# Real 2-D FFT into a squared-ReLU FFN on one Trainium2 core: folds split over two blocks, Nyquist matmuls at the block's end, a row spread by way of DRAM, changed steps by load

## The chip, the cores and the metric

One core of a Trainium2 chip runs the whole kernel. The metric is the device time of one execution in microseconds. Five engines work from queues of their own: TensorE (PE in the profile, its weight loads PEld), VectorE (DVE), ScalarE (ACT), GpSimd (POOL) and SyncE (SP), which issues the stores and the transfer changed here.

## The reference

`x` is 8 x 3008 x 256. The tokens are the real part of its 2-D FFT over sequence and width, and each goes through a feed-forward network with a squared ReLU:

```
X = np.fft.fft(np.fft.fft(x, axis=1), axis=2).real      # 8 x 3008 x 256
t = X.reshape(24064, 256)
h = np.maximum(t @ w_in, 0.0)                           # w_in  256 x 2048
out = (h * h) @ w_out                                   # w_out 2048 x 256
```

## The kernel before

Cosine and sine symmetries shrink the transform. The sequence is folded by VectorE (sums and differences of mirrored rows and columns), and the width transform is multiplied into `w_in` once (`gh`). What is left per batch are the cosine part `zc` and the sine part `zs`, 128 rows each, one column for a pair of mirrored frequencies k and S-k. Of a pair, one token's hidden value is P + Q and the other's P - Q, with P = `gh[:,0]` times `zc` and Q = `gh[:,1]` times `zs`. Row 0 of `zs` is an exception: it carries the component d=128, which enters both tokens with the same sign.

The 12,040 columns are cut into 25 **blocks** (`wins`; counted from 0; 240, 512, 376, 376, 512 and 448 columns, then 512 each, the last 360). A block has eight **steps** of 2 x 128 hidden units. The order of the work is written out by hand, one program order for each engine:

- A **plain step** (`pq`, `square`, `turn`): four matmuls give P + Q in a bank `ph`, ScalarE takes the ReLU, VectorE or (steps in `by_act`) ScalarE squares it into `h2`; two more matmuls with `gh[:,2]` turn the bank into P - Q, and the same follows for the mirrored token.
- A **changed step** (`half_q`, `half_p`, listed by `halved`): two matmuls give Q, ScalarE copies -2Q to `sn`, two matmuls add P, ScalarE copies the sum to `hd`, and VectorE makes P - Q from the two. Row 0's part must not change sign, so VectorE adds back `wv` times `eb`: `eb` is row 0 of `zs` on all 128 partitions, brought by `row_spread` (line 580), which SyncE issues at the head of step 7 of the block before.
- Between the two halves of each step, `others(s)` runs a share of the block before's second matmul (`ffn2_steps`, line 617, sums in `po`, evicted to `osb` at line 632 and stored by SyncE at line 597), of the transform whose columns begin in the next block (`z_steps`, line 481, with the difference `minus` on VectorE, line 497), and the jobs of `at[s]` and `post[s]`.
- The **fold** of batch i >= 2 stands in a **fold block** (`fold_at`: 5, 8, 10, 13, 16, 19): `d_even`, `n_cos`, `d_odd`, `n_sin`, `odds` in steps 0 to 4, then `nyq` (two small matmuls `py`, lines 376 and 377, that read `od` from `odds`) at step 5, `even` (which writes the scratch `scr`) at 6 and `back` (which reads it into `rb`) at 7. `d_odd` also issues the loads of the next batch's `x` on GpSimd. The fold of the odd-even part, `late`, stands in steps 2 to 5 of another block (`late_at`: 6, 9, 12, 15, 18, 21).
- `halved` gives blocks of 512 columns from block 6 on the changed steps 1, 2, 4 and 5, fold blocks 1 and 3; all others none.

Of the kernel before, what the change touches and what calls it, by code (L numbers as in the profile page):

```python
# [9 lines left out]
F16 = mybir.dt.float16  # L10
I32 = mybir.dt.int32
AF = mybir.ActivationFunctionType
ALU = mybir.AluOpType

HS = 32.0
P = 128
# [3 lines left out]
def rev_dim(ap, i):  # L20

    dims = [list(d) for d in ap.ap]
    step, cnt = dims[i]
    dims[i] = [-step, cnt]
    return bass.AP(tensor=ap.tensor, offset=ap.offset + step * (cnt - 1), ap=dims)
# [3 lines left out]
def kernel(  # L29
# [14 lines left out]
    nc = tc.nc  # L44
# [10 lines left out]
    WN = 512  # L55
# [1 line left out]
    FIRST = [240, 512, 376, 376, 512, 448]  # L57
    R23 = float(2.0 ** 23)

    MANY, FEW = (1, 2, 4, 5), (1, 3)  # L60
    SQ_MANY, SQ_FEW = (0, 3, 6), (0, 4, 6)

    RQ = (1, 3, 5, 0, 2, 4)

# [11 lines left out]
    wins = []  # L76
# [5 lines left out]
    NW = len(wins)  # L82
# [29 lines left out]
    drp = ctx.enter_context(tc.tile_pool(name="drp", bufs=2, space=bass.MemoryType.DRAM))  # L112
# [172 lines left out]
    at = const.tile([P, 2, P + 1], F32, name="at")  # L285
# [169 lines left out]
    def zwin(w):  # L455
        if w not in zc:
            zc[w] = zp.tile([P, WN], F16, name="zc", tag="zc")
            zs[w] = zp.tile([P, WN], F16, name="zs", tag="zs")
        return zc[w], zs[w]
# [104 lines left out]
    wv = small([P, NFC], "wv")  # L564
# [8 lines left out]
    eb = {}  # L573

    def row_spread(w):

        wn = wins[w][1]
        t = eb[w] = tmp.tile([P, WN], F16, name="eb", tag="kf")
        src = zwin(w)[1][0:1, 0:wn]
        nc.sync.dma_start(out=t[:, 0:wn], in_=bass.AP(tensor=src.tensor, offset=src.offset, ap=[list(src.ap[0]), [0, P], [1, wn]]))  # L580

    def store(osb, p0, g0, m, minus, eng=nc.sync):

# [65 lines left out]
    folds = {0: f0s}  # L649

    def fold_jobs(i):
        f = folds[i] = fold_steps(i)
        return [f["d_even"], f["n_cos"], f["d_odd"], f["n_sin"], f["odds"], f["nyq"], f["even"], f["back"]]

    fold_at, late_at = {}, {}
# [2 lines left out]
        late_at[win_of(col_of[i, 1]) - 2] = i  # L658
    NST = NFC // 2

    def halved(w):

        if wins[w][1] < WN or w < 6:
            return ()
        return FEW if w in fold_at else MANY

    ROT = [0]
    old = None
    for w in range(NW):
        g0, wn = wins[w]  # L670
        h2 = h2p.tile([P, NFC, 2 * WN], F16, name="h2", tag="h2")
        zcw, zsw = zwin(w)

        lo, hi = 0, NST - 1
        at = [[] for _ in range(NST)]
        post = [[] for _ in range(NST)]
        if w == 0:
            at[2] = [f0s["even"], f0s["back"]]
        elif w == 1:
            fj = fold_jobs(1)  # L680
            at = [[f] for f in fj[0:5]] + [[], [], []]
            post[5] = fj[5:6]
            lo, hi = 6, 7
        elif w == 2:
            te = table_steps(1)
            at = [[folds[1]["even"], lambda: te["freq"](), lambda: te["args"](0)], [lambda: te["turns"](0)], [lambda: te["mods"](0)],
                  [lambda: te["absm"](0)], [lambda: te["sins"](0)], [lambda: te["coss"](0)], [], [lambda: te["weigh"]()]]
            for st in range(4):
                at[st + 3] = at[st + 3] + f0s["late"][st : st + 1]
            at[7].append(folds[1]["back"])  # L690
        elif w in fold_at:
            fj = fold_jobs(fold_at[w])
            at = [[f] for f in fj[0:5]] + [[], fj[6:7], fj[7:8]]
            post[5] = fj[5:6]
        elif w == win_of(col_of[1, 1]) - 1:
            for st in range(4):
                at[st] = folds[1]["late"][st : st + 1]
            lo = 4
        if w in late_at:
            for st in range(4):  # L700
                at[st + 2] = at[st + 2] + folds[late_at[w]]["late"][st : st + 1]
        if w == 3:
            at[0].append(row_weights)
        zj, zl = [], []
        for u in need[w + 1]:
            zu = z_steps(u)
            zj += [(zu, 0, 0), (zu, 1, 0), (zu, 0, 1), (zu, 1, 1)]
        f2 = ffn2_steps(*old) if old else []
        phs = {}

        def pq(s):
            ph = phs[s] = ps_h.tile([P, 2, 512], F32, name="ph", tag="psh")
            for a in range(2):
                f0 = (2 * s + a) * P
                nc.tensor.matmul(ph[:, a, 0:wn], gh[:, 0, f0 : f0 + P], zcw[:, 0:wn], start=True, stop=False)  # L715
                nc.tensor.matmul(ph[:, a, 0:wn], gh[:, 1, f0 : f0 + P], zsw[:, 0:wn], start=False, stop=True)  # L716

        def turn(s):
            for a in range(2):
                f0 = (2 * s + a) * P  # L720
                nc.tensor.matmul(phs[s][:, a, 0:wn], gh[:, 2, f0 : f0 + P], zsw[:, 0:wn], start=False, stop=True, skip_group_check=True)  # L721

        def square(s, sg):
            h1 = h1p.tile([P, 2, 512], F16, name="h1", tag="h1")
            nc.scalar.activation(h1[:, :, 0:wn], phs[s][:, :, 0:wn], AF.Relu)  # L725
            hv = rev_dim(h1[:, :, 0:wn], 2) if sg else h1[:, :, 0:wn]
            if sg == 0 and s in by_act:
                nc.scalar.activation(h2[:, 2 * s : 2 * s + 2, 0:wn], hv, AF.Square)  # L728
            else:
                nc.vector.tensor_tensor(h2[:, 2 * s : 2 * s + 2, sg * wn : (sg + 1) * wn], hv, hv, op=ALU.mult)  # L730

        two = halved(w)
        by_act = () if not two else SQ_FEW if w in fold_at else SQ_MANY
        sns, hds = {}, {}

        def half_q(s):
            ph = phs[s] = ps_h.tile([P, 2, 512], F32, name="ph", tag="psh")
            for a in range(2):
                f0 = (2 * s + a) * P
                nc.tensor.matmul(ph[:, a, 0:wn], gh[:, 1, f0 : f0 + P], zsw[:, 0:wn], start=True, stop=True)  # L740
            i = ROT[0] % 2
            sn = sns[s] = const.tile([P, 2, 2, WN], F16, name=f"sn{i}", tag=f"w16_{i}")
            nc.scalar.activation(sn[:, 0, :, 0:wn], ph[:, :, 0:wn], AF.Copy, bias=0.0, scale=-2.0)  # L743
            for a in range(2):
                nc.vector.tensor_scalar(out=sn[:, 1, a, 0:wn], in0=eb[w][:, 0:wn], scalar1=wv[:, 2 * s + a : 2 * s + a + 1], scalar2=None, op0=ALU.mult)  # L745
            nc.vector.tensor_tensor(sn[:, 0, :, 0:wn], sn[:, 0, :, 0:wn], sn[:, 1, :, 0:wn], op=ALU.add)  # L746

        def half_p(s):
            ph, sn = phs[s], sns[s]
            for a in range(2):  # L750
                f0 = (2 * s + a) * P
                nc.tensor.matmul(ph[:, a, 0:wn], gh[:, 0, f0 : f0 + P], zcw[:, 0:wn], start=False, stop=True, skip_group_check=True)  # L752
            hd = tmp.tile([P, 2, 2 * WN], F16, name="hd", tag=("tt", "tm")[ROT[0] % 2])
            ROT[0] += 1
            nc.scalar.activation(hd[:, :, 0:wn], ph[:, :, 0:wn], AF.Copy, bias=0.0, scale=1.0)  # L755
            nc.vector.tensor_tensor(rev_dim(hd[:, :, wn : 2 * wn], 2), hd[:, :, 0:wn], sn[:, 0, :, 0:wn], op=ALU.add)  # L756
            nc.vector.tensor_scalar(out=hd, in0=hd, scalar1=0.0, scalar2=None, op0=ALU.max)  # L757
            nc.vector.tensor_tensor(h2[:, 2 * s : 2 * s + 2, :], hd, hd, op=ALU.mult)  # L758

        def others(s):  # L760
            for j in at[s]:
                j()
            for j in spread(f2, s, NST):
                j()
            for j in post[s]:
                j()
            if s == lo:
                zl[:] = [j for zu, part, h in zj for j in zu(part, h)]
            if s >= lo:
                for j in spread(zl, s - lo, hi - lo) if s < hi else []:  # L770
                    j()


        ng = 2 if w == 0 or wins[w - 1][1] < 384 < wn else 1
        for s0 in range(0, NST, ng):
            ss = range(s0, s0 + ng)
            if s0 == hi and w + 1 < NW and halved(w + 1):
                row_spread(w + 1)
            if s0 in two:
                half_q(s0)  # L780
                others(s0)
                half_p(s0)
                continue
            for s in ss:
                pq(s)
            for s in ss:
                square(s, 0)
            others(s0)
            for s in ss:
                turn(s)  # L790
            for s in ss:
                square(s, 1)
            for s in ss[1:]:
                others(s)
        old = (w, h2)
    for j in ffn2_steps(*old, tail=True):
        j()
# [30 lines left out]
```

## Time and profile before

| | |
|---|---|
| median of 3 runs | 635.52 us (635.35 to 637.25) |
| profiled execution | 632.15 us, span 630.0 us, mean granted TensorE clock 0.992 |
| busy: PE, ACT, DVE, POOL | 596.5, 511.2, 475.5, 80.8 us |
| matmuls `po` (L617) | 3024 |
| plain steps, changed steps | 138, 62 |
| transfers | 49.89 MB, mean 79 GB/s |

Matmuls overlap in the profile, so their busy time and their mean duration are longer than the distance from one start to the next. A bracket at the end of a timeline row gives the engine's idle time before it and what ended it. "A <- B" in the table of waits says that A stood idle until B was done. In the windows view each row is a stretch of the span: its length, the busy time of each engine with the number of instructions, the granted clock, the share of the DMA engines and their rate.

### The profile page before, as it was taken

The page shows a single profiled execution, that of the slowest core. Times are in us where ns is not written, and L with a number is a line of the kernel's source. Part 1 is how long each engine was busy: PE and PEld are TensorE (multiplying, and loading weights), DVE is VectorE, ACT ScalarE, POOL GpSimd, SP SyncE. Part 2 cuts the span into 40 slices and gives each one's busy share as a digit, 9 for nine tenths or more (in the row PEclk, how much of TensorE's full clock was granted, in tenths as well). Part 3 has the DMA queues.
Part 4 walks back from the last instruction along what each step waited for, and adds up shares of the span by engine and source line. Part 5 has one row for each costly group of instructions (what it writes and reads, how often), then busy time and mean ns, then how long its engine had stood idle before and what let it go on. Part 6 is the DMA issues. An engine that isn't in the chain of part 4 may idle for free.

```text
span 630.0 us, 11638 instructions
## 1 busy us (share of the span) xinstructions
PE 596.5 (95%) x4440; PEld 428.5 (68%) x4440; DVE 475.5 (75%) x799; ACT 511.2 (81%) x664; POOL 80.8 (13%) x125
## 2 busy tenths in 40 slices
PE   5899999999899999899999999999996999999997
PEld 2457786776577677577776777766774677777786
DVE  7887655766799688867997779959787587886830
ACT  7787778779798888789888898888896689899762
POOL 5352200022000210210003200022000200000000
PEclk9999999999999999899999999999999899999999
DMA  8936211174313823743137533264322313413112
GB/s 148 211 80 129 85 34 34 50 142 110 31 54 57 169 80 52 144 92 57 52 45 116 136 59 42 61 119 122 49 39 68 72 65 43 55 49 39 58 53 66
DMA packets 39118, 49.89 MB, mean 79 GB/s; under 512 B 4503, under 2 KB 32919, under 8 KB 39063
## 3 DMA queue, kind: packets, MB, share of 16 engines
q1 hardware_dynamic: 29491, 26.80, 22.2%
q0 software_dynamic: 9344, 22.14, 17.4%
q8 instruction: 34, 0.56, 0.4%
q10 hardware_dynamic: 228, 0.21, 0.1%
q14 instruction: 21, 0.17, 0.1%
HBM read 33.63 MB, written 27.84 MB: 98 GB/s over the span
## 4 chain that ended last, share of the span: by engine, by line
PE 51%; DVE 19%; ACT 11%; issue 8%; DMA 8%; POOL 2%; ACTq 0%; DVEq 0%; POOLq 0%
PE po L617 29%; ACT h L725 5%; PE ph L721 5%; PE ph L715 5%; PE ph L716 5%; DVE h L730 3%; PE ph L752 3%; DVE h L758 3%; DMA out_dram<-osb 3%; DMA eb<-zs 2%; PE ph L740 2%; DVE hd L757 2%; DVE hd L756 2%; PE pz L481 2%; DVE fo L356 2%
## 5 line engine op out<-in xcount | busy, mean ns | idle before, releaser
L617 PE MATMUL po<-wout,h 128*128 128x256 f16 (+1 forms) x3024 | 363.2, 273 | 0.0
L617 PEld LDWEIGHTS <-h 128*128 128x128 f16 (+1 forms) x3024 | 297.6, 99 | 72.6 <-issue 1.1
L725 ACT ACTIVATE h<-ph 128x1024 f16<-128x1024 f32 (+4 forms) x276 | 253.2, 951 | 46.6 <-PE ph L721 31.5
L730 DVE TENSOR_TENSOR h<-h 128x1024 f16<-128x1024 f16 (+4 forms) x222 | 137.1, 632 | 93.0 <-ACT h L725 89.6
L716 PE MATMUL ph<-zs,gh 128*128 128x512 f16 (+4 forms) x276 | 99.9, 364 | 3.1 <-DVE zs L497 2.7
L715 PE MATMUL ph<-zc,gh 128*128 128x512 f16 (+4 forms) x276 | 99.9, 364 | 1.1 <-ACT h L725 0.8
L721 PE MATMUL ph<-zs,gh 128*128 128x512 f16 (+4 forms) x276 | 76.7, 363 | 1.9 <-ACT h L725 1.5
L632 ACT ACTIVATE osb<-po 128x512 f32<-128x512 f32 (+3 forms) x95 | 54.7, 579 | 29.3 <-PE po L617 27.0
L755 ACT ACTIVATE hd<-ph 128x1024 f16<-128x1024 f32 x62 | 63.6, 1026 | 17.3 <-PE ph L752 17.1
L758 DVE TENSOR_TENSOR h<-hd 128x2048 f16<-128x2048 f16 x62 | 76.0, 1226 | 2.1
L743 ACT ACTIVATE sn<-ph 128x1024 f16<-128x1024 f32 x62 | 63.6, 1025 | 0.0
L728 ACT ACTIVATE h<-h 128x1024 f16<-128x1024 f16 x54 | 57.1, 1057 | 1.7
L756 DVE TENSOR_TENSOR hd<-hd,sn 128x1024 f16<-128x1024 f16 x62 | 42.7, 688 | 10.0 <-ACT hd L755 8.2
L715 PEld LDWEIGHTS <-gh 128*128 128x128 f16 x276 | 27.1, 98 | 30.9 <-issue 4.8
L746 DVE TENSOR_TENSOR sn<-sn 128x1024 f16<-128x1024 f16 x62 | 42.9, 692 | 6.8 <-DVE sn L745 0.5
L745 DVE TENSOR_SCALAR sn<-eb,wv 128x512 f16<-128x512 f16 x124 | 38.1, 350 | 12.5 <-DMA eb<-zs 12.5
L716 PEld LDWEIGHTS <-gh 128*128 128x128 f16 x276 | 27.1, 98 | 29.6 <-issue 3.6
L757 DVE TENSOR_SCALAR hd<-hd 128x2048 f16<-128x2048 f16 x62 | 43.0, 694 | 2.1
L752 PE MATMUL ph<-zc,gh 128*128 128x512 f16 x124 | 36.8, 378 | 2.5 <-ACT sn L743 2.0
L740 PE MATMUL ph<-zs,gh 128*128 128x512 f16 x124 | 36.9, 379 | 0.0
L721 PEld LDWEIGHTS <-gh 128*128 128x128 f16 x276 | 25.6, 98 | 8.9 <-issue 3.9
L424 POOL COPY xt<-xt 128x2 f16<-128x2 f16 x16 | 5.2, 352 | 173.4 <-DVE xt L407 89.1
(121 smaller groups left out, 371.4 us busy)
## 6 DMA issues: line engine op xcount, KB each, us to landing
out_dram<-osb SPq DMA_DIRECT2D x77, 128.0 KB
xo<-in_x_dram POOLq DMA_DIRECT2D x7, 768.0 KB, 7.8
scr<-ev POOLq DMA_DIRECT2D x8, 390.0 KB, 5.2
eb<-zs SPq DMA_DIRECT2D x18, 128.0 KB
rb<-scr POOLq DMA_DIRECT2D x16, 130.0 KB, 3.9
out_dram<-osb SPq DMA_DIRECT2D x12, 94.0 KB
w<-in_moe_w_in_dram POOLq DMA_DIRECT2D x2, 512.0 KB, 10.2
wout<-in_moe_w_out_dram POOLq DMA_DIRECT2D x1, 1024.0 KB, 14.6
```

What stands on the lines that cost most here:

```text
L617: nc.tensor.matmul(po[0:m, j * D : (j + 1) * D], h2[:, fc, q : q + m], wout16[:, fc, :], start=(fc == 0), stop=(fc == NFC - 1))
L715: nc.tensor.matmul(ph[:, a, 0:wn], gh[:, 0, f0 : f0 + P], zcw[:, 0:wn], start=True, stop=False)
L716: nc.tensor.matmul(ph[:, a, 0:wn], gh[:, 1, f0 : f0 + P], zsw[:, 0:wn], start=False, stop=True)
L721: nc.tensor.matmul(phs[s][:, a, 0:wn], gh[:, 2, f0 : f0 + P], zsw[:, 0:wn], start=False, stop=True, skip_group_check=True)
L725: nc.scalar.activation(h1[:, :, 0:wn], phs[s][:, :, 0:wn], AF.Relu)
L728: nc.scalar.activation(h2[:, 2 * s : 2 * s + 2, 0:wn], hv, AF.Square)
L730: nc.vector.tensor_tensor(h2[:, 2 * s : 2 * s + 2, sg * wn : (sg + 1) * wn], hv, hv, op=ALU.mult)
L743: nc.scalar.activation(sn[:, 0, :, 0:wn], ph[:, :, 0:wn], AF.Copy, bias=0.0, scale=-2.0)
L752: nc.tensor.matmul(ph[:, a, 0:wn], gh[:, 0, f0 : f0 + P], zcw[:, 0:wn], start=False, stop=True, skip_group_check=True)
L755: nc.scalar.activation(hd[:, :, 0:wn], ph[:, :, 0:wn], AF.Copy, bias=0.0, scale=1.0)
L757: nc.vector.tensor_scalar(out=hd, in0=hd, scalar1=0.0, scalar2=None, op0=ALU.max)
L758: nc.vector.tensor_tensor(h2[:, 2 * s : 2 * s + 2, :], hd, hd, op=ALU.mult)
```

## The change

- `PLAN` and `plan` choose the changed steps of a block by its load: a fold block counts 2, a block that holds the first part of a fold or a late fold 1 each. Load 0 gets four changed steps, 1 gets three, 2 or more gets two. Blocks 3, 5 and 24 get changed steps too; in all there are 61.
- The fold goes over two blocks: `d_even` and `n_cos` in steps 0 and 2 of the block before the fold block (`first_at`: 4, 7, 9, 12, 15, 18), then `d_odd` at 0, `n_sin` at 2, `odds` at 3, `even` at 5, `back` at 6, and `nyq` after step 7's matmuls. The late fold moves to steps 3 to 6. `row_weights` moves from block 3 to block 2.
- `row_spread` stores row 0 of `zs` to a DRAM scratch `zr` and then reads it from there onto 128 partitions.
- In a changed step the VectorE instructions on `sn` and `eb` come after `others` and after the copy to `hd`.

```diff
--- before.py
+++ after.py
@@ -57,8 +57,7 @@
     FIRST = [240, 512, 376, 376, 512, 448]
     R23 = float(2.0 ** 23)
 
-    MANY, FEW = (1, 2, 4, 5), (1, 3)
-    SQ_MANY, SQ_FEW = (0, 3, 6), (0, 4, 6)
+    PLAN = {4: ((1, 2, 4, 5), (0, 3, 6)), 3: ((1, 3, 5), (2, 4, 6)), 2: ((1, 4), (0, 3, 6)), 0: ((), ())}
 
     RQ = (1, 3, 5, 0, 2, 4)
 
@@ -576,8 +575,10 @@
 
         wn = wins[w][1]
         t = eb[w] = tmp.tile([P, WN], F16, name="eb", tag="kf")
-        src = zwin(w)[1][0:1, 0:wn]
-        nc.sync.dma_start(out=t[:, 0:wn], in_=bass.AP(tensor=src.tensor, offset=src.offset, ap=[list(src.ap[0]), [0, P], [1, wn]]))
+        zr = drp.tile([1, WN], F16, name="zr", tag="zr")
+        nc.sync.dma_start(out=zr[0:1, 0:wn], in_=zwin(w)[1][0:1, 0:wn])
+        src = zr[0:1, 0:wn]
+        nc.sync.dma_start(out=t[:, 0:wn], in_=bass.AP(tensor=src.tensor, offset=src.offset, ap=[[0, P], [1, wn]]))
 
     def store(osb, p0, g0, m, minus, eng=nc.sync):
 
@@ -658,13 +659,23 @@
         late_at[win_of(col_of[i, 1]) - 2] = i
     NST = NFC // 2
 
+    first_at = {}
+    for w, i in fold_at.items():
+        first_at[w - 1] = i
+
+    def plan(w):
+
+        if w < 3 or w == 4:
+            return PLAN[0]
+        load = 2 * (w in fold_at) + (w in first_at) + (w in late_at)
+        return PLAN[(4, 3, 2)[min(load, 2)]]
+
     def halved(w):
 
-        if wins[w][1] < WN or w < 6:
-            return ()
-        return FEW if w in fold_at else MANY
+        return plan(w)[0]
 
     ROT = [0]
+    jobs_of = {}
     old = None
     for w in range(NW):
         g0, wn = wins[w]
@@ -689,18 +700,22 @@
                 at[st + 3] = at[st + 3] + f0s["late"][st : st + 1]
             at[7].append(folds[1]["back"])
         elif w in fold_at:
-            fj = fold_jobs(fold_at[w])
-            at = [[f] for f in fj[0:5]] + [[], fj[6:7], fj[7:8]]
-            post[5] = fj[5:6]
+            fj = jobs_of.pop(fold_at[w])
+            at = [fj[2:3], [], fj[3:4], fj[4:5], [], fj[6:7], fj[7:8], []]
+            post[7] = fj[5:6]
         elif w == win_of(col_of[1, 1]) - 1:
             for st in range(4):
                 at[st] = folds[1]["late"][st : st + 1]
             lo = 4
         if w in late_at:
             for st in range(4):
-                at[st + 2] = at[st + 2] + folds[late_at[w]]["late"][st : st + 1]
-        if w == 3:
-            at[0].append(row_weights)
+                at[st + 3] = at[st + 3] + folds[late_at[w]]["late"][st : st + 1]
+        if w in first_at:
+            fj = jobs_of[first_at[w]] = fold_jobs(first_at[w])
+            at[0] = at[0] + fj[0:1]
+            at[2] = at[2] + fj[1:2]
+        if w == 2:
+            at[2].append(row_weights)
         zj, zl = [], []
         for u in need[w + 1]:
             zu = z_steps(u)
@@ -730,7 +745,7 @@
                 nc.vector.tensor_tensor(h2[:, 2 * s : 2 * s + 2, sg * wn : (sg + 1) * wn], hv, hv, op=ALU.mult)
 
         two = halved(w)
-        by_act = () if not two else SQ_FEW if w in fold_at else SQ_MANY
+        by_act = plan(w)[1]
         sns, hds = {}, {}
 
         def half_q(s):
@@ -741,9 +756,6 @@
             i = ROT[0] % 2
             sn = sns[s] = const.tile([P, 2, 2, WN], F16, name=f"sn{i}", tag=f"w16_{i}")
             nc.scalar.activation(sn[:, 0, :, 0:wn], ph[:, :, 0:wn], AF.Copy, bias=0.0, scale=-2.0)
-            for a in range(2):
-                nc.vector.tensor_scalar(out=sn[:, 1, a, 0:wn], in0=eb[w][:, 0:wn], scalar1=wv[:, 2 * s + a : 2 * s + a + 1], scalar2=None, op0=ALU.mult)
-            nc.vector.tensor_tensor(sn[:, 0, :, 0:wn], sn[:, 0, :, 0:wn], sn[:, 1, :, 0:wn], op=ALU.add)
 
         def half_p(s):
             ph, sn = phs[s], sns[s]
@@ -753,9 +765,13 @@
             hd = tmp.tile([P, 2, 2 * WN], F16, name="hd", tag=("tt", "tm")[ROT[0] % 2])
             ROT[0] += 1
             nc.scalar.activation(hd[:, :, 0:wn], ph[:, :, 0:wn], AF.Copy, bias=0.0, scale=1.0)
+            for a in range(2):
+                nc.vector.tensor_scalar(out=sn[:, 1, a, 0:wn], in0=eb[w][:, 0:wn], scalar1=wv[:, 2 * s + a : 2 * s + a + 1], scalar2=None, op0=ALU.mult)
+            nc.vector.tensor_tensor(sn[:, 0, :, 0:wn], sn[:, 0, :, 0:wn], sn[:, 1, :, 0:wn], op=ALU.add)
             nc.vector.tensor_tensor(rev_dim(hd[:, :, wn : 2 * wn], 2), hd[:, :, 0:wn], sn[:, 0, :, 0:wn], op=ALU.add)
-            nc.vector.tensor_scalar(out=hd, in0=hd, scalar1=0.0, scalar2=None, op0=ALU.max)
-            nc.vector.tensor_tensor(h2[:, 2 * s : 2 * s + 2, :], hd, hd, op=ALU.mult)
+            hv = hd[:, :, 0 : 2 * wn]
+            nc.vector.tensor_scalar(out=hv, in0=hv, scalar1=0.0, scalar2=None, op0=ALU.max)
+            nc.vector.tensor_tensor(h2[:, 2 * s : 2 * s + 2, 0 : 2 * wn], hv, hv, op=ALU.mult)
 
         def others(s):
             for j in at[s]:
@@ -792,6 +808,8 @@
                 square(s, 1)
             for s in ss[1:]:
                 others(s)
+            if s0 + 1 == hi and ng > 1 and w + 1 < NW and halved(w + 1):
+                row_spread(w + 1)
         old = (w, h2)
     for j in ffn2_steps(*old, tail=True):
         j()
```

## The prediction

> **What bounds the kernel now.** I read the page first: engines and granted clock.
>
> ```profile
> span 630.0 us, 11638 instructions
> PE 596.5 (95%) x4440; PEld 428.5 (68%) x4440; DVE 475.5 (75%) x799; ACT 511.2 (81%) x664; POOL 80.8 (13%) x125
> PEclk9999999999999999899999999999999899999999
> ```
>
> TensorE is busy for 95% of the span, so time goes only through fewer matmul columns or through what is left of the other 5%. The clock shows two slices with an 8, near 260 and 495 us: TensorE stood still there and ran slowly afterwards. So next I cut the span at the first `ph` matmul of each block (blocks counted from 0; these are 7, 8, 10, 12, 13, 19, 21, 23).
>
> ```profile
> core 0: us, PE busy (x) PEld busy (x) DVE busy (x) ACT busy (x) POOL busy (x), PEclk, DMA share, GB/s
> 164.02:191.16 27.14, 24.21 (x190) 17.69 (x190) 22.10 (x37) 22.04 (x30) 0.20 (x2) 1.00 0.31 45
> 191.16:216.28 25.12, 23.86 (x175) 16.87 (x174) 22.38 (x35) 20.76 (x24) 3.99 (x4) 1.00 0.66 116
> 241.06:270.11 29.05, 26.70 (x196) 18.63 (x195) 23.62 (x37) 22.38 (x30) 3.99 (x4) 0.94 0.58 105
> 294.88:317.94 23.06, 22.85 (x170) 16.41 (x169) 18.97 (x33) 20.46 (x24) 1.37 (x4) 1.00 0.34 53
> 317.94:343.69 25.75, 24.85 (x195) 18.05 (x194) 23.60 (x35) 22.21 (x30) 4.23 (x5) 1.00 0.51 92
> 465.06:498.39 33.33, 27.24 (x195) 19.04 (x194) 23.62 (x35) 22.49 (x30) 1.77 (x4) 0.90 0.30 56
> 523.17:546.22 23.05, 22.84 (x169) 16.41 (x168) 18.86 (x33) 20.45 (x24) 1.38 (x4) 1.00 0.31 50
> 570.52:593.57 23.05, 22.84 (x170) 16.41 (x169) 17.76 (x29) 20.45 (x24) 0.00 (x0) 1.00 0.29 52
> ```
>
> Blocks 10, 13 and 19 are fold blocks with the same matmuls, yet take 29.05, 25.75 and 33.33 us. Blocks 12, 21 and 23 have hardly any idle TensorE. The table of waits names what stops the others:
>
> ```profile
> engine line waited for: us in total, times, longest us
> DVE sn L745 <- DMA eb<-zs: 12.5, 6, 5.3
> PE py L376 <- DVE od L371: 12.4, 6, 6.1
> PE ph L716 <- DVE zs L497: 2.7, 1, 2.7
> ```
>
> The `py` matmuls wait at step 5 of a fold block for `od`, at the end of a VectorE queue that holds the whole fold (busy 23.6 of 25.75 us in block 13). Where the broadcast row `eb` is late as well, that queue has stood still before. The timeline, TensorE then VectorE, shows the waits one by one:
>
> ```profile
> 46.69 0.18 PE L376 MATMUL py<-od,perm 128*128 128x1 f16 x1 [0.99 <-DVE od L371]
> 261.53 0.16 PE L376 MATMUL py<-od,perm 128*128 128x1 f16 x1 [2.32 <-DVE od L371]
> 336.79 0.16 PE L376 MATMUL py<-od,perm 128*128 128x1 f16 x1 [0.90 <-DVE od L371]
> 489.11 0.16 PE L376 MATMUL py<-od,perm 128*128 128x1 f16 x1 [6.09 <-DVE od L371]
> 490.36 0.63 PE L715 MATMUL ph<-zc,gh 128*128 128x512 f16 x1
> 490.79 0.63 PE L716 MATMUL ph<-zs,gh 128*128 128x512 f16 x1
> 570.52 0.38 PE L715 MATMUL ph<-zc,gh 128*128 128x512 f16 x1
> 570.73 0.38 PE L716 MATMUL ph<-zs,gh 128*128 128x512 f16 x1
> ...
> 475.61 0.61 DVE L745 TENSOR_SCALAR sn<-eb,wv 128x512 f16<-128x512 f16 x2 [5.26 <-DMA eb<-zs]
> 576.95 0.62 DVE L745 TENSOR_SCALAR sn<-eb,wv 128x512 f16<-128x512 f16 x2 [1.44 <-DMA eb<-zs]
> ```
>
> A 512-column matmul starts 0.215 us after the one before (570.52 to 570.73), but 0.43 us after it (490.36 to 490.79) behind the long wait: half speed.
>
> **The change part by part.**
>
> *The `py` matmuls at step 7, the fold over two blocks.* Of the 12.4 us of waits for `od`, the 1.0 of block 1 stays (its jobs are not moved); 11.4 us lie in blocks 8, 10, 13, 16 and 19. `od` is now written from step 3, its reader comes in step 7. Four steps of about 3 us are 12 us of room; the longest lateness was 6.1. So I take all 11.4 off. The slow clock goes with the waits. Block 10 is 3.30 longer than block 13, and its wait 2.32 - 0.90 = 1.42 longer: 1.88 left over. Block 19 is 7.58 longer, its wait 5.19: 2.39 left over. Together **-4.3 us**, and the waits **-11.4 us**.
>
> [...]
>
> What moves: `d_even` and `n_cos` go one block ahead, into blocks 4, 7, 9, 12, 15 and 18; `d_odd`, with its loads of the next batch, from step 2 to step 0. VectorE's prices are these.
>
> ```profile
> L758 DVE TENSOR_TENSOR h<-hd 128x2048 f16<-128x2048 f16 x62 | 76.0, 1226 | 2.1
> L756 DVE TENSOR_TENSOR hd<-hd,sn 128x1024 f16<-128x1024 f16 x62 | 42.7, 688 | 10.0 <-ACT hd L755 8.2
> L746 DVE TENSOR_TENSOR sn<-sn 128x1024 f16<-128x1024 f16 x62 | 42.9, 692 | 6.8 <-DVE sn L745 0.5
> L745 DVE TENSOR_SCALAR sn<-eb,wv 128x512 f16<-128x512 f16 x124 | 38.1, 350 | 12.5 <-DMA eb<-zs 12.5
> L757 DVE TENSOR_SCALAR hd<-hd 128x2048 f16<-128x2048 f16 x62 | 43.0, 694 | 2.1
> L730 DVE TENSOR_TENSOR h<-h 128x1024 f16<-128x1024 f16 (+4 forms) x222 | 137.1, 632 | 93.0 <-ACT h L725 89.6
> L352 DVE TENSOR_TENSOR fe<-xo 128x3072 f16<-128x3072 f16 x8 | 14.3, 1786 | 1.8 <-DMA xo<-in_x_dram,idx_r 1.6
> L361 DVE TENSOR_TENSOR ab<-fe 128x1560 f16<-128x1560 f16 x8 | 7.7, 964 | 0.0
> ```
>
> A changed step costs VectorE 1226 + 688 + 692 + 2 x 350 + 694 = 4.0 us, a plain one two squares, 1.3: 2.7 more. Block 12 gains 1.79 + 0.96 = 2.75 of fold (two small copies aside) and gives up two changed steps, 5.4: 18.97 - 2.65 = 16.3 busy of about 24. The fold blocks keep two changed steps and lose 2.75. So no block is left with VectorE near its length; I cost the move at nothing. If that cover went, `zs` would be late as it now is in block 7 (below).
>
> The loads of `x` go out two steps earlier on GpSimd, ahead of `scr` and `rb` as before, and nothing is moved past them; the shortest distance from a load to its reader falls from nearly two blocks to one, block 8 to block 9, some 24 us. Nothing. Behind the `py` read at step 7 VectorE holds only the last square of the block, and the next `po` needs the other bank, whose eviction has had a half step. Nothing; up to 0.5 us a fold block if not, 3 in all.
>
> *The wait at block 7's start* (2.7): four changed steps and the late fold of one batch fill block 6. It gets three, with the late fold a step later. VectorE is relieved by 2.7 there, and `zs` was late by 2.7. I take **-2.7**; the other end is 0.
>
> *Changed steps by load.* A changed step has two 512-column matmuls fewer, 2 x 0.215 = 0.43 us. Blocks 9, 12, 15, 18 lose two each and 6, 7, 21 one: 11 x 0.43 = +4.7. Block 3 (376 columns) gets four, block 5 (448) two, block 24 (360) four: 0.43 x (4 x 376 + 2 x 448 + 4 x 360) / 512 = -3.2. Net **+1.5 us**. Those three blocks have room on VectorE. `row_weights`, which the changed steps of block 3 need, goes from block 3 to block 2 with the same 16 one-column matmuls: nothing.
>
> *The row by way of DRAM.* The wait added is SyncE's, for `zr` to land, with the stores behind it, and VectorE's for `eb`, at the same first changed step as now: only the halved step's own chain is put after `others`. The transfers nearest to it:
>
> ```profile
> scr<-ev POOLq DMA_DIRECT2D x8, 390.0 KB, 5.2
> rb<-scr POOLq DMA_DIRECT2D x16, 130.0 KB, 3.9
> 467.46 0.90 SPq L580 DMA_DIRECT2D eb<-zs  x1
> ```
>
> Today `eb` took from 467.46 to 475.61, 8.15 us. The new pair is bounded above by `scr` plus `rb`, 9.1 us (the first moves 390 KB there and 1 KB here), below by one of them, 3.9. I take about 6: the second is nearest to `rb`, the first has almost no bytes. Then `eb` comes no later than now, and the cost is 0, from -1 (less idle VectorE) to +3. Block 23 shows the cover: its VectorE waited 1.44 us for `eb`, and it took 23.05 us, like block 21.
>
> [...]
>
> **Sum:** -11.4 - 4.3 - 2.7 + 1.5 = -16.9 us. The profiled execution took 632.15 us (span 630.0) and would take 615.3. It lies 3.4 below the median of the runs, 635.52; from the median it is 618.6. I predict **618 us**.
>
> **The rivals.**
>
> *The row is still late (15%).* At 467 us SyncE was late for want of a free queue behind stores, which stay, and then waits once more for `zr`. If blocks 10 and 19 again lose VectorE 2 to 5 us, plain squares back up and TensorE waits, perhaps 2 to 4 us a block with the slow clock: 622 to 627. Against: `py` no longer hangs on it.
>
> *The backlog goes a block ahead (8%).* If `d_even` and the late fold in blocks 7, 9, 12, 15 and 18 push `zs` back, the next block starts with block 7's 2.7: 5 x 2.7 = 13.5, or 632. The VectorE sums above speak against it.
>
> *The DRAM pair is slow: slower than before (6%).* SyncE waits for `zr` in 21 blocks, with two to three us a block now taken from stores, and `eb` lands late in all. It decides from 16.9 / 21 = 0.8 us of TensorE wait per block; at 1.2 us it is 618.6 + 25.2 = 644. Since 1.44 us of VectorE waiting was free, the pair would have to take about 2.6 us more than the present one, near 11 us: over both bounds.
>
> That the change does nothing is no rival: nearly all of the sum hangs on where `py` stands in TensorE's order.
>
> **How the numbers follow.** Forecast 69% (612 to 622: median or profiled level, block 7's 2.7 and the 3 us of `py`), late row 15%, backlog 8%, slow pair 6%, and 2% for anything that lands within 0.3%, about what a measurement of this kernel can tell from no change. The range, 611 to 627, holds the first two; slower 6%, same 2% and faster 92%.
>
> **What would show it.** Right: no row of `py` waiting for `od` but block 1's; no 8 in the clock row; blocks 10, 13, 16 and 19 equal, near 24.8 us; blocks 12 and 15 near 23.9; `eb` under 7 us from its first issue. Wrong: TensorE waiting for `zs` or for an activation at blocks' starts, waits for `eb` in most blocks, or stores that hold up `osb`.

## The result and the profile after

| | before | after |
|---|---|---|
| median of 4 runs each | 636.38 us (635.35 to 638.06) | 626.19 us (624.99 to 627.99) |
| ratio, 95% interval | | 0.984 (0.9805 to 0.9875) |
| profiled execution, span | 632.15, 630.0 us | 627.99, 626.1 us |

The change made the kernel 10 us (1.6%) faster. I had forecast about 17; 626 lies at the upper end of the range, outside the forecast's own 612 to 622 and where the first rival had been put. The two profiled executions, from which all block lengths come, lie only 4.2 us apart: the one before is below its median, the one after is the slowest of its four. The page's engines and clock of the kernel after:

```profile
span 626.1 us, 11668 instructions
PE 597.8 (95%) x4442; PEld 428.7 (68%) x4442; DVE 466.2 (74%) x786; ACT 517.9 (83%) x673; POOL 77.3 (12%) x125
PEclk9999999999999999999999999999899999999999
...
DVE sn L769 <- DMA eb<-zr: 17.3, 4, 7.3
PE ph L764 <- ACT sn L758: 8.8, 17, 2.5
PE py L375 <- DVE od L370: 1.0, 1, 1.0
```

`py` waits in block 1 alone: 11.4 us of waits are gone, as forecast. But `eb` is waited for 17.3 us instead of 12.5, in four places instead of six, and there is still an 8 in the clock. The same cut by blocks (7, 10, 12, 13, 17, 18, 19) says where:

```profile
core 0: us, PE busy (x) PEld busy (x) DVE busy (x) ACT busy (x) POOL busy (x), PEclk, DMA share, GB/s
164.35:188.77 24.42, 24.37 (x192) 17.86 (x190) 20.33 (x34) 21.85 (x30) 0.00 (x0) 1.00 0.18 48
238.43:263.59 25.16, 24.86 (x195) 18.11 (x194) 18.96 (x28) 22.20 (x30) 3.27 (x4) 1.00 0.54 123
288.38:312.28 23.90, 23.63 (x173) 16.80 (x172) 19.22 (x31) 20.43 (x24) 0.72 (x4) 1.00 0.16 48
312.28:337.44 25.16, 24.86 (x195) 18.11 (x194) 19.00 (x28) 22.20 (x30) 3.88 (x5) 1.00 0.60 126
411.29:438.05 26.76, 24.84 (x182) 17.60 (x181) 14.95 (x28) 22.10 (x30) 3.08 (x4) 1.00 0.25 73
438.05:466.47 28.42, 25.72 (x174) 17.27 (x172) 23.06 (x37) 20.59 (x24) 0.73 (x4) 0.94 0.15 38
466.47:495.48 29.01, 26.53 (x195) 18.76 (x194) 18.87 (x28) 22.43 (x30) 1.67 (x3) 0.94 0.21 63
```

Block 7 fell from 27.14 to 24.42 and block 10 from 29.05 to 25.16. Block 12 grew from 23.06 to 23.90, the two changed steps given up. All these are close to the forecast. Blocks 17, 18 and 19 are not: 26.76, 28.42 and 29.01 us, where their like take 24.78 (block 14), 23.90 and 25.16. That is 2.0 + 4.5 + 3.9 = 10.4 us. The timelines show the chain there (start, length, engine, instruction; in brackets the wait before it). First SyncE:

```profile
405.21 8.74 SPq L598 DMA_DIRECT2D out_dram<-osb  x5
414.06 0.22 SPq L579 DMA_DIRECT2D zr<-zs  x1
420.47 0.35 SPq L581 DMA_DIRECT2D eb<-zr  x1
```

VectorE:

```profile
423.73 0.62 DVE L769 TENSOR_SCALAR sn<-eb,wv 128x512 f16<-128x512 f16 x2 [7.29 <-DMA eb<-zr]
```

TensorE:

```profile
427.11 0.59 PE L764 MATMUL ph<-zc,gh 128*128 128x512 f16 x2 [0.90 <-ACT sn L758]
431.22 0.59 PE L764 MATMUL ph<-zc,gh 128*128 128x512 f16 x2 [1.02 <-ACT sn L758]
441.36 0.61 PE L618 MATMUL po<-wout,h 128*128 128x256 f16 x4 [1.19 <-DVE h L774]
443.08 0.39 PE L618 MATMUL po<-wout,h 128*128 128x256 f16 x2 [1.11 <-DVE h L745]
```

SyncE spent 405.2 to 414.0 on five stores, so `zr` was issued 2.8 us into block 17 (in the kernel before, `eb`'s one transfer went out 2.6 us ahead of that block). `zr` then took 6.4 us for 1 KB, and the row from DRAM 3.3. VectorE stood 7.3 us, ScalarE waited 2.1 us in block 17 for VectorE to be done with `sn`'s buffers, TensorE lost 1.9 us in block 17 and more at the head of block 18, where `h2` was not ready. In block 19 VectorE waited 5.4 us for the row; there SyncE had come to it late in the kernel before, too (467.46, 2.4 us into the block). What else moved while `zr` was in flight in block 19 (468.45 to 474.08)?

```profile
468.70:474.00 5.30, 5.30 (x43) 3.83 (x42) 2.17 (x2) 4.95 (x7) 0.00 (x0) 1.00 0.07 24
```

A DMA share of 0.07 at 24 GB/s is as much as one of the 16 engines busy all the time (0.07 x 16 = 1.1; the view gives the share, not the engine). So the theory tested first, theory Q in the expectations below: **the row waits for one crowded DMA engine**. Ahead of block 19's row SyncE stores 113, 79, 79 and 113 rows, counts that are prime; from 456.0 to 468.6 us the DMA moved 23 or 26 GB/s in 29 of 40 equal slices, about the rate of the row's own wait. From these rates comes the author's estimate that such a store keeps to one engine and that the single row has to pass there too; no view names the engine of a transfer. Against it stood: the way by DRAM is slow by itself; or VectorE's backlog was only handed on.

### The profile page after: what moved, and what is told of

The parts are those of the page before. It is cut to its first block, busy times and chain, and to the rows that moved or that the text cites. A ratio compares the mean times of both kernels' runs of the same rounds, so it can differ in the third digit from the quotient of the medians.

```text
span 626.1 us, 11668 instructions
## 1 busy us (share of the span) xinstructions
PE 597.8 (95%) x4442; PEld 428.7 (68%) x4442; DVE 466.2 (74%) x786; ACT 517.9 (83%) x673; POOL 77.3 (12%) x125
## 4 chain that ended last, share of the span: by engine, by line
PE 67%; ACT 13%; DVE 8%; issue 6%; DMA 4%; POOL 1%; ACTq 0%; SPq 0%; DVEq 0%; POOLq 0%
PE po L618 38%; ACT h L740 7%; PE ph L730 7%; PE ph L731 7%; PE ph L736 7%; PE ph L764 4%; ACT sn L758 3%; PE ph L755 2%; PE pz L480 2%; ACT osb L633 2%; DVE h L745 1%; DVE h L774 1%; DMA w<-in_moe_w_in_dram 1%; DMA eb<-zr 1%; ACT es L485 1%
## 5 line engine op out<-in xcount | busy, mean ns | idle before, releaser
L767 ACT ACTIVATE hd<-ph 128x1024 f16<-128x1024 f32 (+3 forms) x61 | 60.4, 990 | 16.4 <-PE ph L764 16.3
L774 DVE TENSOR_TENSOR h<-hd 128x2048 f16<-128x2048 f16 (+3 forms) x61 | 72.1, 1182 | 2.1
L743 ACT ACTIVATE h<-h 128x1024 f16<-128x1024 f16 (+3 forms) x63 | 64.8, 1029 | 2.0
L758 ACT ACTIVATE sn<-ph 128x1024 f16<-128x1024 f32 (+3 forms) x61 | 60.3, 989 | 2.1 <-DVE hd L771 2.1
L771 DVE TENSOR_TENSOR hd<-hd,sn 128x1024 f16<-128x1024 f16 (+3 forms) x61 | 40.9, 671 | 22.5 <-ACT hd L767 18.7
L769 DVE TENSOR_SCALAR sn<-eb,wv 128x512 f16<-128x512 f16 (+3 forms) x122 | 36.6, 343 | 17.4 <-DMA eb<-zr 17.3
L770 DVE TENSOR_TENSOR sn<-sn 128x1024 f16<-128x1024 f16 (+3 forms) x61 | 40.9, 671 | 5.6
L764 PE MATMUL ph<-zc,gh 128*128 128x512 f16 (+3 forms) x122 | 35.1, 369 | 9.1 <-ACT sn L758 8.8
L773 DVE TENSOR_SCALAR hd<-hd 128x2048 f16<-128x2048 f16 (+3 forms) x61 | 41.0, 672 | 2.1
L755 PE MATMUL ph<-zs,gh 128*128 128x512 f16 (+3 forms) x122 | 35.7, 374 | 0.0
```

Source lines behind the costliest of these rows:

```text
L774: nc.vector.tensor_tensor(h2[:, 2 * s : 2 * s + 2, 0 : 2 * wn], hv, hv, op=ALU.mult)
```

## The experiments

The kernel before ran beside each of the three groups of four: 634.40, 633.38 and 634.60 us median. Times are medians.

**The stores evened**, after the change (shortened: these lines take the place of the one store):

```diff
+            k = max(k for k in range(1, 17) if cnt % k == 0)
+            cuts = [(0, cnt)] if cnt <= 16 or k > 4 else [(0, cnt // 16 * 16), (cnt // 16 * 16, cnt)]
+            for c, e in cuts:
+                eng.dma_start(... rows c to e ...)
```

> The changed kernel with its stores cut anew: a store of more than 16 rows whose count has no divisor from 5 to 16 goes as two, a multiple of 16 rows and the rest. Row transfers stay as they are. Theory Q: the packets in a row of 0.046 us each at 405 to 419 us come from stores such as 113, 79 and 53 rows that run on one DMA engine; cut, they spread, the waits of the row in blocks 17 and 19 go, and the time falls by about 10 us to 616 to 619. Rival R (the way by DRAM): no change in the waits for eb. Rival S (SyncE's issuing is the bound): more stores make it worse, by some 0.3 us each on SyncE, and the row comes later.

616.59 us, ratio 0.972 (0.9664 to 0.9775). Blocks 17, 18 and 19:

```profile
412.01:436.79 24.78, 24.68 (x182) 17.60 (x180) 18.77 (x34) 21.98 (x30) 3.19 (x4) 1.00 0.25 73
436.79:460.69 23.90, 23.63 (x173) 16.83 (x172) 19.23 (x31) 20.43 (x24) 0.73 (x4) 1.00 0.16 50
460.69:485.85 25.16, 24.86 (x195) 18.10 (x194) 18.96 (x28) 22.20 (x30) 0.58 (x1) 1.00 0.20 62
```

SyncE's timeline ahead of block 17:

```profile
410.43 0.22 SPq L579 DMA_DIRECT2D zr<-zs  x1
411.85 0.35 SPq L581 DMA_DIRECT2D eb<-zr  x1
```

The three blocks have the lengths of their like, and `eb` follows `zr` after 1.4 us instead of 6.4. Nothing about the row was touched, so the shape of the stores is what makes the row late, and the row's path is not slow by itself. Even stores give more than that: blocks 5 and 24 are 1.0 and 1.2 us shorter as well.

**The row on another queue**: `nc.sync` to `nc.gpsimd` for both of its transfers, after the change.

> The changed kernel with both transfers of the row issued by GpSimd, on its queue, and not by SyncE. Theory Q (the row waits in SyncE's queue behind stores that drain one packet of 1 KB after another): blocks 17, 18 and 19, which took 26.75, 28.42 and 29.01 us after the change, come to the lengths of their like, 24.8, 23.9 and 25.2 us, no 8 is left in the clock row, and the time falls by some 10 us from the changed kernel's profiled 627.99 us, to 616 to 619. Rival R (the way by DRAM is slow by itself, whoever issues it): VectorE still waits for eb in blocks 17 and 19, for 3 us or more, and the time stays within 3 us of the changed kernel's. Rival P (GpSimd has its own waits before that point, for scr and for the late fold's copies): eb is late in other blocks, and new gaps show there.

650.27 us, ratio 1.0274 (1.0208 to 1.034). Rival P, and worse than it said:

```profile
DVE sn L769 <- DMA eb<-zr: 51.1, 10, 8.7
POOL eb L581 <- DMA zr<-zs: 44.5, 17, 5.0
```

In blocks 17 and 20 GpSimd comes to the row only after its wait for `scr` and four issues of `rb`, and it waits 2.6 us on average for each `zr`. This kernel also prices a late row: with 51.1 us of VectorE waiting its profiled execution is 22 us longer than that of the changed kernel with its 17.3.

**The row spread from SBUF again**, after the change:

```diff
-        nc.sync.dma_start(out=zr[0:1, 0:wn], in_=zwin(w)[1][0:1, 0:wn])
-        src = zr[0:1, 0:wn]
+        src = zwin(w)[1][0:1, 0:wn]
```

> The changed kernel with the row spread by one transfer from SBUF, as in the kernel before. It tells what the way by DRAM is worth in the changed schedule. By theory Q the one transfer has 16 engines and only its share on the crowded one, and SyncE has no wait for a first transfer: eb comes some 2 us earlier after its issue in blocks 17 and 19 than the pair of 8.5 to 9.7 us did, and the time is 2 to 5 us below the changed kernel's. By the rival that the way by DRAM brings a gain (the transfer from one partition took 6.5 to 8.2 us in all blocks), eb is late in more blocks and the time 2 us or more above it.

621.72 us, ratio 0.9801 (0.9745 to 0.9858): 4.5 us under the changed kernel, as theory Q said. With stores as they are, the way by DRAM is a loss. Blocks 17, 18 and 19:

```profile
411.93:436.71 24.78, 24.68 (x181) 17.59 (x180) 15.66 (x29) 21.98 (x30) 3.08 (x4) 1.00 0.40 81
436.71:463.02 26.31, 24.30 (x173) 16.61 (x172) 22.22 (x36) 20.53 (x24) 0.73 (x4) 1.00 0.21 39
463.02:489.88 26.86, 24.85 (x195) 18.11 (x194) 18.84 (x28) 22.31 (x30) 0.59 (x1) 1.00 0.36 68
```

So 4.1 of the 10.4 us stay without the way by DRAM. SyncE still comes to the row 2.5 and 2.2 us into blocks 17 and 19, and VectorE waits 4.5 and 4.9 us for it.

**The way by DRAM alone**, the reverse edit on the kernel before:

> The kernel before with one edit: the row goes by way of DRAM. Theory Q (a transfer of one row runs on one DMA engine, the one that the stores of 113, 79, 59 or 53 rows run on too): in quiet blocks the pair takes about 1.2 + 3 us, less than the 6.5 to 7 of the single transfer, but behind those stores it takes 8 to 10, so VectorE's wait in block 19 (5.3 us before) becomes 5 to 8 and block 17 is late as well; since py still waits for od at step 5, each shows in the time: 636 to 645 us, no better than before. If the way by DRAM is a gain in this schedule, the waits for eb (12.5 us before) fall under 6 and the time under 632.

636.72 us, ratio 1.0042 (1.0015 to 1.0069), 3.3 us above the kernel before that ran beside it, as theory Q said. The waits for `eb` rise from 12.5 to 19.9 us (7.1, 5.3 and 6.0 of them in blocks 11, 17 and 19) and the longest for `od` from 6.1 to 6.9:

```profile
DVE sn L747 <- DMA eb<-zr: 19.9, 6, 7.1
PE py L376 <- DVE od L371: 11.8, 6, 6.9
```

**The stores evened before the change**:

> The kernel before with evened stores and nothing else. Theory Q: eb is late in block 19 no more and block 19 falls from 33.33 us to the 25.75 of block 13, some 7.5 us; block 10, where zs was late by VectorE's own backlog, keeps most of its 29.05. The time falls by 7 to 9 us to 626 to 628. What is then left to the change itself, against the changed kernel with evened stores (616.6), is 10 us: the waits of py (about 1 us in each of blocks 8, 13, 16, 19, 2.3 in 10 with the slow clock), block 7's 2.7 and the changed steps in 3, 5 and 24. Rival: store shapes don't matter before the change, within 2 us of before.

621.33 us, ratio 0.9782 (0.9743 to 0.9821): 12 us, more than the 7 to 9 expected and more than the change itself. Blocks 10 and 19:

```profile
240.03:269.08 29.05, 26.69 (x195) 18.59 (x194) 23.62 (x37) 22.48 (x30) 5.08 (x6) 0.94 0.63 111
464.03:489.73 25.70, 24.85 (x195) 18.05 (x194) 23.54 (x35) 22.14 (x30) 0.58 (x1) 1.00 0.31 62
```

Block 19 lost its 7.6 us, block 10 kept its 29.05. Of the rest, 2 us lie in block 7 (25.19) and 1.2 in the tail. With even stores the whole change is worth 621.33 - 616.59 = 4.7 us (3.9 by the two ratios).

**`py` after step 7 alone**, on the kernel before (`post[5]` to `post[7]`):

> The kernel before with one edit: the py matmuls after step 7's matmuls and not after step 5's. My prediction gave -11.4 us to the waits for od and -4.3 us to the slow clock behind them, both by py's place together with the split fold. If py's place alone does it, the 11.4 us go and the time falls by 13 to 16 us, more than the whole change brought. If VectorE's backlog is only handed on, py no longer waits but TensorE waits for zs, for h2 or for ScalarE at the next block's start, and the time falls by less than 6 us.

629.07 us, ratio 0.9927 (0.9896 to 0.9958): half of the change's gain. The 5.3 us lie just inside the second expectation (under 6), though the profiled execution, the fastest of ten with 624.74, does not. Blocks 12, 13 and 19:

```profile
288.34:313.49 25.15, 23.45 (x169) 16.25 (x168) 21.84 (x38) 20.53 (x24) 1.37 (x4) 1.00 0.31 48
313.49:338.30 24.81, 24.81 (x195) 18.12 (x194) 23.25 (x34) 22.50 (x30) 3.31 (x4) 1.00 0.53 93
459.69:491.18 31.49, 26.69 (x196) 18.88 (x195) 23.62 (x35) 22.43 (x30) 0.59 (x1) 0.95 0.33 59
```

In a quiet fold block (13) TensorE no longer stops at all, with VectorE as full as before: nothing is handed on. What is left lies where the row is late: block 19 takes 31.49 instead of 33.33, and block 12 grew from 23.06 to 25.15, after VectorE had waited 4.0 us for `eb` in block 11. `py` had been where the late row showed, not why.

**Both on the kernel before**, even stores and `py` after step 7:

> The kernel before with evened stores and the py matmuls after step 7, nothing else: no split fold, no way by DRAM, the old choice of changed steps. With py alone moved, blocks 13 and 16 took 24.81 and 24.75 us against 25.16 after the whole change, and 12 and 15 can take 23.05 against 23.91. If the split and the choice by load only cost steps where py waits no longer, this takes 614 to 618 us, as the changed kernel with evened stores or better, though blocks 3, 5 and 24 have no changed steps (3.2 us). If the split is what keeps VectorE from holding TensorE up, blocks 7, 10 and 12 show waits for zs and h2, and it takes 620 or more.

615.34 us, ratio 0.9693 (0.9657 to 0.9729). That is 6.0 us under even stores alone, where the whole change brought 4.7. Blocks 7, 10, 12 and 13:

```profile
166.85:192.28 25.43, 24.20 (x189) 17.71 (x188) 20.69 (x35) 22.15 (x30) 0.00 (x0) 1.00 0.32 45
240.76:267.17 26.41, 25.15 (x195) 18.15 (x194) 23.18 (x36) 22.61 (x30) 3.99 (x4) 1.00 0.64 120
291.95:315.00 23.05, 22.84 (x169) 16.42 (x168) 18.86 (x33) 20.44 (x24) 1.37 (x4) 1.00 0.35 54
315.00:339.81 24.81, 24.81 (x196) 18.12 (x194) 23.23 (x34) 22.42 (x30) 4.37 (x5) 1.00 0.51 94
```

Block 12 keeps its four changed steps (23.05 against 23.90 after the change) and block 13 is shorter (24.81 against 25.16). Only blocks 7 and 10 still wait.

**The old choice of changed steps**, in the changed kernel with even stores:

> The changed kernel with evened stores (616.6 us) and the old choice of changed steps (1, 2, 4, 5 in blocks from 6 on, 1 and 3 in fold blocks, none in 3, 5 and 24). By my step price of 0.43 us blocks 9, 12, 15 and 18 gain 0.86 each and 6, 7, 21 gain 0.43, 4.7 us, and blocks 3, 5, 24 lose 3.2: 615 us if VectorE keeps up. If it doesn't (a changed step costs it 2.7 us more than a plain one, and these blocks hold the first part of a fold and a late fold: 19 + 5.4 us of VectorE work in 23), zs or h2 is late at the next block's start, up to 2.7 us in each of five blocks, with slow clock behind it: 620 to 630.

619.24 us, ratio 0.9758 (0.9722 to 0.9793), 2.6 over the choice by load: between the two cases. Blocks 12 and 13:

```profile
290.07:313.12 23.05, 22.84 (x169) 16.40 (x168) 20.74 (x35) 20.44 (x24) 0.41 (x2) 1.00 0.18 55
313.12:339.24 26.12, 25.19 (x196) 17.88 (x195) 22.24 (x33) 22.14 (x30) 6.71 (x9) 1.00 0.52 116
```

And a row of its waits:

```profile
PE po L621 <- DVE h L747: 2.8, 3, 0.9
```

Block 12 gains its 0.85 and hands 1.0 to block 13, where `po` waits for `h2`. So beside the split fold the old choice gains nothing. But it loses little either: of the 3.8 us by which the blocks of this run are longer than with the choice by load, 2.6 lie in blocks 3, 5 and 24, which have no changed steps here, and 1.2 in blocks 6 to 23.

**After the change, once more**:

> The changed kernel as it is, on the chip of this call, for the comparisons. Theory Q: 624 to 628 us, with VectorE waiting for eb in blocks 17 and 19 again, since the order and the shapes of the stores are fixed; only how far the crowded engine is behind may differ. If the late row were chance, other blocks or none would show it.

628.59 us, ratio 0.9898 (0.9852 to 0.9945), with blocks 17, 18 and 19 at 27.0, 28.3 and 29.2 us: the late row is in the program, not chance.

**Even stores and the row from SBUF**, after the change:

> The changed kernel with evened stores (616.6 us) and the row spread by one transfer from SBUF. It prices the way by DRAM where no crowded engine disturbs it. The pair took about 1.1 us to zr's landing and at most 3 behind it, the single transfer 6.5 to 7; but in the changed kernel the row is asked for 7.5 to 9 us after its issue in most blocks, so only blocks 5, 7 and 23, where it is issued late, can tell: 616 to 618 us, within 1.5 us of the pair. If the single transfer's load on all 16 engines delays stores or x, 619 or more.

616.18 us, ratio 0.971 (0.9667 to 0.9752), level with 616.59. With even stores the way by DRAM neither gains nor loses.

**What the runs point to**: the kernel before, even stores, `py` after step 7, changed steps also in blocks 3 and 24, three of them in blocks 6 and 9, and `row_weights` in block 2. Of the edit, the line with the choice:

```diff
-        return FEW if w in fold_at else MANY
+        return FEW if w in fold_at else THREE if w in (6, 9) else MANY
```

> What the runs point to: the kernel before with evened stores and py after step 7 (615.3 us), four changed steps in blocks 3 and 24, three (1, 3, 5) in blocks 6 and 9, which hold a late fold and the transform of an even part and after which TensorE waited (block 7 took 25.44 and block 10 26.41 us there). No split fold and no way by DRAM. Blocks 3 and 24 give 0.8 and 1.0 (as measured in the changed kernel with evened stores), block 7 about 1.0 and block 10 about 1.6, less 0.43 in each of 6 and 9: 611 to 613 us, under both kernels and under every run so far. If the waits after blocks 6 and 9 only move on, 613 to 616.

611.30 us, ratio 0.9645 (0.961 to 0.968). The page:

```profile
PE 590.7 (97%) x4428; PEld 426.2 (70%) x4428; DVE 482.9 (79%) x817; ACT 515.9 (85%) x670; POOL 80.9 (13%) x125
PEclk9999999999999999999999999999999999999999
```

Blocks 7 and 10:

```profile
164.29:188.58 24.29, 24.05 (x189) 17.68 (x188) 18.53 (x33) 22.04 (x30) 0.00 (x0) 1.00 0.34 48
237.22:262.03 24.81, 24.81 (x195) 18.11 (x194) 21.40 (x31) 22.43 (x30) 3.99 (x4) 1.00 0.65 123
```

In this execution TensorE is busy for 97% of the span and never slowed. With the way by DRAM on top:

> The version of the run before this one with the row by way of DRAM. With evened stores the pair should bring eb 2 to 3 us earlier than the single transfer, which matters only where eb was waited for (1 to 1.6 us in blocks 6, 7 and 10, where no TensorE time hung on it): within 1 us of it. If SyncE's wait for zr holds up stores, 1 us or more above.

611.35 us, ratio 0.9641 (0.9598 to 0.9684): the same.

## Why the prediction was right, and where its sum was off

The range held, but the mechanism of the forecast held only in part: the time fell where the first rival had been put, and the forecast of 618 missed by 8.

- **Waits of `py`, -11.4**: right in amount, half right in cause. They went. But the 5.2 us by which block 19's wait exceeded block 13's came from the late row; even stores alone took block 19 from 33.33 to 25.70, `py`'s place alone only to 31.49. And the split fold, which I credited together with `py`'s place, adds nothing in a quiet fold block: 24.81 us with `py` alone moved, 25.16 with all.
- **Slow clock, -4.3**: block 10's part went (25.16, clock 1.00). Block 19's came back by another door, in blocks 18 and 19, each with a mean clock of 0.94.
- **Block 7, -2.7**: right in amount (24.42 against 27.14 - 2.7 + 0.43 = 24.87), but the cause, VectorE's relief in block 6, is not shown. Three runs that leave block 6's changed steps and its late fold as they were bring block 7 down nearly as far: 24.83 with `py` alone moved, 25.03 with the way by DRAM alone, 25.19 with even stores alone. With even stores and `py` moved, three changed steps in block 6 were worth 1.15 (25.44 to 24.29).
- **Changed steps by load, +1.5**: nearer +3. Blocks 9, 12 and 15 grew by 0.9 each, as forecast, block 21 not at all. Blocks 3, 5 and 24 gave less than the 3.2 of the sum: block 3 fell by 0.8 while block 2, with `row_weights`, grew by 0.4, block 24 fell by 1.1, and block 5 grew by 0.4. Block 5's row is the last job of block 4, it went out 1.5 us into block 5, and VectorE waited 3.6 us for it: 23.5 us instead of 22.4.
- **The move of the fold, 0**: about +0.4 us in each of blocks 10, 13 and 16, against a forecast near 24.8. TensorE waits 0.3 us there for ScalarE's copy to `sn` (a part of the 8.8 us of `PE ph L764`, 2.0 before; 4.4 of it are in blocks 17 and 19); I had put the cost on VectorE alone. The second changed step of these blocks moved from step 3 to 4 as well; which of the two does it was not tried.
- **The row by way of DRAM, 0 (bounds -1 to +3): the term that was mis-sized.** It measured +4.5 by the medians (626.19 against 621.72 with the row from SBUF), some 6.2 in blocks 17 to 19. My 6 us for the pair were near with even stores (5.7 us in block 5), but the bounds were medians over a whole run and say nothing about one transfer behind uneven stores: in block 17 it took 9.7 us.
- **The row is still late, rival at 15%: the case that came.** The other 4.1 us of blocks 17 to 19 are there whichever way the row goes. I had written that SyncE was late "for want of a free queue behind stores, which stay" (the last store ahead of the row held SyncE for 4.33 us in the kernel before, from 463.03), priced it at 2 to 4 us a block in two blocks, and left it out of the sum. With both, 618.6 from the median plus 10.4 is 629.0, and 626.2 to 628.6 was measured. With even stores the changed kernel measures 616.6, 1.4 under the forecast; that is partly luck, since the 2.2 us that even stores save in blocks 5 and 24 stand in no term.
- **The backlog goes a block ahead, rival at 8%**: it didn't with the choice by load, and did with the old choice (1.0 us in block 13).

One thing stays open: why SyncE reached block 17's row 5.4 us later than in the kernel before. It is not the pair: with the row from SBUF in the changed schedule it was as late (2.5 us into the block), and with the pair in the kernel before it went out 2.6 us ahead of the block, as before. What differs is GpSimd's loads of `x`, which the change issues two steps earlier and which I had priced at "nothing". The 6.2 us ahead of the five stores, after and before the change:

```profile
399.00:405.20 6.20, 5.89 (x48) 4.40 (x47) 4.21 (x9) 5.27 (x9) 2.65 (x2) 1.00 0.95 145
403.93:410.13 6.20, 5.55 (x44) 4.08 (x43) 6.03 (x10) 5.88 (x9) 1.16 (x1) 1.00 0.48 81
```

The DMA engines were busy for 95% of that time instead of 48%. Whether that holds the stores back was not tried by itself; even stores were enough to bring the row out 1.6 us ahead of the block.

## What to carry to other kernels

Before pricing a small transfer by its bytes, look at the transfers ahead of it: here 1 KB took 6.4 us behind uneven stores and 1.4 us behind even ones (block 17), and a DMA share near 1/16 (0.07 in block 19) while an engine waited was the sign of it. A wait that differs between blocks of equal work (0.9, 2.3, 6.1 us) can have a second cause besides the one that the row names; look for it first, since here removing it was worth more (12 us) than the change. And moving the reader later (`py` by two steps) did, with even stores, what splitting the writer's work over two blocks was to do, without costing changed steps (615.3 against 616.6 us).

## What the runs showed of the hardware that was not expected

TensorE's clock halved without any single long idle: in block 18 after the change the two longest waits were 1.19 and 1.11 us, yet from 443.45 on the granted clock was 0.50 for 3.41 us. Of the slow stretches in the profiles before and after, those that end within the span lie at 261.94 (3.41 us) and 487.22 (6.83 us) before, and at 443.45 and 484.41 (3.41 us each) after. Here are, in block 18 after the change, the 3.42 us ahead of the slow stretch and the slow one; then, in the kernel before, 3.41 us with most of block 7's wait of 2.69 us, and the 3.41 us ahead of the slow stretch of block 10, with its wait of 2.32 us.

```profile
440.03:443.45 3.42, 1.11 (x8) 0.52 (x7) 3.39 (x7) 0.93 (x1) 0.00 (x0) 1.00 0.48 115
443.45:446.86 3.41, 3.29 (x13) 1.74 (x12) 3.37 (x7) 3.09 (x4) 0.00 (x0) 0.50 0.00 0
163.00:166.41 3.41, 1.40 (x10) 0.76 (x9) 3.34 (x7) 1.94 (x3) 0.31 (x2) 1.00 0.13 38
258.53:261.94 3.41, 1.09 (x13) 0.81 (x11) 3.34 (x6) 1.05 (x2) 0.92 (x1) 1.00 1.04 194
```

TensorE was busy for 1.11 and 1.09 us of the two stretches that a slow one followed. Block 7's wait was longer than block 10's and than those of block 18, yet the clock stayed at 1.00. So in these traces the length of one wait does not tell whether the clock halves; what does was not shown.

Where VectorE waited for the row, the spread of one SBUF partition to 128 arrived 6.5 to 9.3 us after its issue in the kernel before, and 6.0 to 8.7 us in the runs with even stores. The pair by way of DRAM, with even stores, was waited for in two places: 5.7 us after the issue of `zr` in block 5 of the changed kernel, and 8.6 us in block 17 of the last run.
